# When queries are turned and multiplied by the tangent, in a linear-attention and Swish kernel: two steps moved, and five smaller pieces of work shared out anew

## The chip, the cores and the metric

The kernel runs on one core of one Trainium2 chip. The metric is device time in microseconds for one execution. Before the change the median of 5 runs is 277.74 us (277.08 to 279.45).

## What is computed

Attention without a softmax, then a feed-forward layer with a Swish whose slope is given per feature. Cut to what matters:

```python
# q, k, v: (8 batches, 8 heads, 576 positions, 64), w_in 512x2048, w_out 2048x512
theta = np.pi / 2.0 * pos / S                 # c = cos(theta), s = sin(theta)
phi = lambda x: np.concatenate([relu(x) * c, relu(x) * s], axis=-1)
q_p, k_p = phi(q), phi(k)
kv = np.einsum('bhsf,bhsd->bhfd', k_p, v);  z = np.sum(k_p, axis=2)
num = np.einsum('bhsf,bhfd->bhsd', q_p, kv)
den = np.einsum('bhsf,bhf->bhs', q_p, z)[..., None] + 1e-06
x = (num / den)                               # laid out as (4608 tokens, 512)
h = x @ w_in
g = h * (1.0 / (1.0 + np.exp(-beta * h)))
out = g @ w_out
```

The kernel takes the cosine out of num and den, so that a query needs only its ReLU and, for the second half of the features, its ReLU times the tangent.

## The kernel before, in words

The 4608 tokens are nine chunks c of 512; the attention works by batches b of 576 tokens. While chunk c goes through the feed-forward layer, the attention of batch b = c + 1 is finished, and its result becomes part of the input of the next chunk. The products with `w_in` and `w_out` are mostly done in the seven-product form for two by two blocks (`h_fast` at L459 and `o_fast` at L534), which needs sums of blocks beforehand: `g_sum` (L390, tiles S) over the activations, `wh_sums` (L439) over blocks of `w_in`, `x_sum` (L901) over blocks of the chunk's input.

Each engine runs its own queue in program order and waits on semaphores. No scheduler reorders anything: the order is that of the Python calls. In chunks 3 to 8 it is a list written out by hand, `ORDER` (L874) for chunks 3 to 6, read word by word by `chunk` (L930). Words that matter here:

- `c5X` is VectorE's copy of a partial product (L494); `kt` its copy of the key-value product into `kv` (L284); words with `a`, such as `a2Y` or `a3Y`, are VectorE's additions in PSUM (L496 to L498); `SaX`, `SbV` and the like are ScalarE's Swish activations of a pair of feature blocks (L413).
- `s01` to `s34` are VectorE's S sums (L399).
- `N0` is TensorE's numerators of batch b (L293), then `x0` to `x2` divide them (L304 to L315) and turn the result with a transposing DMA on SyncE's queue (L363).
- `q0` and `q1` are the ReLU of the queries of batch b + 2 into the one buffer `qb` (L194). `k`, `v` and `w` words are the ReLU of keys and the products of values by sine (ScalarE, L217) and cosine (VectorE, L219) for batch b + 1.
- `g0` and `g1` are GpSimd's two tangent products (L222, `q_tan`): the queries turned by DMA, `qts[b % 2]`, times the tangent.
- The queries of a batch are turned by one DMA of 18 blocks of 128x128, issued by SyncE (L252, `q_turn_dma`). It reads `qb` and writes `qts[b % 2]`.

GpSimd's queue also issues the stores of the output (L510, `store`), and SyncE's queue all loads (L79), the query turns and the turns of x.

Chunks 0 and 1 are a plain loop over 16 feature blocks (slots) with side work hung on slots (`early`, L736, and the loop at L809). Chunk 2 has its own order (`h_first`, L989, and the loop body from L1012), and ends with products named by `x[...]` and `y[...]`, where `y["a7"]` is VectorE's addition at L599 and `y["4"]` the last product, which goes on in the PSUM bank that `a7` reads.

The seven products of one pair in `o_fast` use three PSUM banks, and each is waited for by ScalarE's or VectorE's copy of what it left:

```python
"7": lambda: prod(b_ps, s_part(S3), T3, False, False, late(c)),
"4": lambda: prod(b_ps, g_part(1, 1), T4, False, True, late(c)),
"c1": lambda: nc.scalar.copy(p1, b_ps),
"a7": stored("2a7", lambda: nc.vector.tensor_tensor(o2[:, HM:DM], b_ps, p5, **add)),
```

Of the kernel before, what the change touches and what calls it, by code (L numbers as in the profile page):

```python
# [17 lines left out]
NQ = 9  # L18
# [4 lines left out]
def kernel(  # L23
# [14 lines left out]
    nc = tc.nc  # L38
# [154 lines left out]
        else:  # L193
            nc.vector.tensor_scalar(dst, src, scalar1=0.0, scalar2=None, op0=ALU.max)  # L194

    def q_relu(b, jp, eng="dve"):
        relu(qb[:, jp].rearrange("q n (j d) -> q j n d", j=2), raw_tile(b, "q")[:, 2 * jp : 2 * jp + 2], eng)

    def k_relu(b, j0=0, j1=4, eng="dve", n0=0, n1=NQ):
        relu(rk.rearrange("q n j d -> q j n d")[:, j0:j1, n0:n1], raw_tile(b, "k")[:, j0:j1, n0:n1], eng)  # L200
# [47 lines left out]
    def qs_of(b):  # L248
        return wx["q"] if b > 3 and b % 2 == 0 else qs_first

    def q_turn_dma(b):
        nc.sync.dma_start(out=qts[b % 2].rearrange("q s n c -> q (s n) c"),  # L252
                          in_=qb.rearrange("q s n c -> q (s n c)"), transpose=True)

    def q_tan(b, jp, behind=None):
        got = tan_mul(nc.gpsimd, qs_of(b)[:, jp], qts[b % 2][:, jp], 0, NQ)

        if behind is not None:
            tc.add_manual_dep(got.ins, behind.ins.name,
                              mybir.DependencyInfo(mybir.DependencyClass.Sync, mybir.DependencyReason.DATA),  # L260
                              reason="GpSimd behind the sums")

    def kv_out(jp, bank):
        return ps[:, bank : bank + 2, jp * 2 * E : (jp + 1) * 2 * E]
# [120 lines left out]
    def h_act(c, jt):  # L385
        if (c, jt // 4) not in gs:
            gs[c, jt // 4] = gt_pool.tile([P, 4, TCH], BF16, name="g_t", tag="g_t")
        nc.scalar.activation(gs[c, jt // 4][:, jt % 4], ps[:, h_bank(c, jt)], AF.Silu, scale=beta[:, jt : jt + 1])  # L388

    def g_sum(c, i0, i1, kind):  # L390

# [13 lines left out]

    def h_group(c, jt, cols=1):
        h_mm(c, jt, cols=cols)
        h_act(c, jt)

    def h_silu(c, jt, bank):  # L410
        if (c, jt // 4) not in gs:
            gs[c, jt // 4] = gt_pool.tile([P, 4, TCH], BF16, name="g_t", tag="g_t")
        nc.scalar.activation(gs[c, jt // 4][:, jt % 4], ps[:, bank], AF.Silu, scale=beta[:, jt : jt + 1])  # L413

    def h_plain(c, jt, bank, cols=1):
        xt = xt_tile(c)
# [276 lines left out]
    def rest():  # L693

        cast_halves(2)
        cast_halves(3)
        x_mul(x_rden(2, 0, 8, NQ, (0, 1)), 8, NQ)
        load_w("out", 0)
        load_w("out", 1)
        load_raw(1, "v")  # L700
        load_raw(1, "k")
        load_raw(1, "q")
        load_w("out", 2, 2)
        load_w("out", 3, 2)
        x_turn_dma(0, 8, 9)
        for j in range(8):
            cast_out(j)
        v_scale(1, 0)
        k_relu(1)
        q_relu(1, 0)  # L710
        q_relu(1, 1)


    def num_seven(jp, bank):
# [5 lines left out]
    def second():  # L720
# [14 lines left out]

    early = {  # L736
        4: lambda: (num_mm(0, 8, 0, 2, 0), num_mm(0, 8, 1, 2, 1), rest()),
        15: lambda: v_scale(1, 1, eng="act"),
        22: lambda: (kv_mm(1, 0, 6), kv_mm(1, 1, 6), kv_take((0, 1), 6, "act")),
        23: second,  # L740
        25: lambda: (num_seven(0, 4), x_mul(x_rden(4, 0, 0, 7, (0,)), 0, 7), cast_out(13)),
        26: lambda: (num_seven(1, 6), x_mul(x_rden(6, 0, 0, 7, (1,)), 0, 7)),
# [28 lines left out]
        if b + 1 < B:  # L771
            load_raw(b + 1, "k")

    def kv_all(b, bank=6):
        kv_mm(b, 0, bank)
        kv_mm(b, 1, bank)
        kv_take((0, 1), bank)

    def x_part(b, t, bank):
        x_div(t, bank)  # L780
# [30 lines left out]
    for slot in range(16):  # L811
        h_group(1, slot)
        if slot == 0:
            num_rest()
            att_q(2)
            v_half(2, 0)
        if 3 <= slot < NQ:
            v_half(2, 1, slot, slot + 1, "act")
        if slot == 4:
            k_all(2)  # L820
            v_half(2, 1, 0, 3)
        elif slot == 6:
            w_sums()
        elif slot == 11:
            kv_all(2)
            for jp in range(2):
                tan_mul(nc.vector, qs_of(2)[:, jp], qts[0][:, jp], 0, NQ)
    q_relu(3, 0, "act")
# [38 lines left out]
    def k_piece(b, j):  # L867
# [4 lines left out]
            load_raw(b + 1, "k")  # L872

    ORDER = (  # L874
# [6 lines left out]
    ORDER_LAST = (  # L881
# [42 lines left out]
    def chunk(c, b, x, y, parts):  # L924
        steady = {"X": (0, 2, 0, 1), "Y": (4, 3, 4, 5), "Z": (8, 0, 2, 1), "V": (12, 4, 3, 5)}
        end = {"X": (0, 6, 0, 1), "E": (2, 5, 3, 4), "Y": (4, 2, 0, 1), "F": (6, 7, 3, 4), "Z": (8, 6, 0, 1),
               "V": (12, 5, 3, 4)}
        pairs = {n: h_fast(c, at[0], at[1:]) for n, at in (steady if b < B else end).items()}

        def plain_bank(n):  # L930
            return (2 if n == 7 else 6 + n % 2) if b < B else (2, 7)[n % 2]

        plain = [2, 3, 6, 7, 10, 11, 14, 15]
        outs = {"x": x, "y": y}

        def q_next():
            if b + 3 < B:
                load_raw(b + 3, "q")

        def raw_next(name):  # L940
            if b + 2 < B:
                load_raw(b + 2, name)

        xs_all = {"x0", "x1", "x2"}
        take = prep(b, [
            ({"k0", "k1", "k2", "k3"} | xs_all, lambda: raw_next("k")),
            ({"q0", "q1"} | xs_all, q_next),
            ({f"{o}{n}" for o in "vw" for n in range(NQ)}, lambda: raw_next("v"))])
        last_sum = None
        for op in (ORDER if b < B else ORDER_END if c + 1 < NTC else ORDER_LAST).split():  # L950
            n = int(op[-1]) if op[-1].isdigit() else None
            if op == "K":
                kv_mm(b, 0, 4)
                kv_mm(b, 1, 4)
            elif op == "kt":
                kv_take((0, 1), 4)
            elif op[0] == "N":
                for t, bank in enumerate(parts):
                    num_all(b, t, bank)
            elif op[0] == "x":  # L960
                x_part(b, n, parts[n])
                take(op)
            elif op[0] in "kvwq":
                take(op)
            elif op[0] == "t":
                if c + 1 < NTC:
                    x_sum(c + 1, n)
            elif op[0] == "g":
                if b + 1 < B:
                    q_tan(b + 1, n, None if n else last_sum)  # L970
            elif op[0] == "p":
                h_plain(c, plain[n], plain_bank(n), 2 if n < SPLITS.get(c, (0, 0))[0] else 1)
            elif op[:2] == "sp":
                h_silu(c, plain[n], plain_bank(n))
            elif op[0] == "o" and n is not None:
                outs[op[1]][op[2]]()
            elif op[0] == "o":
                outs[op[2]]["a" + op[1]]()
            elif op[0] == "c" and op[2] in "xyo":
                outs["x" if op[2] == "o" else op[2]][op[:2]]()  # L980
            elif op[0] == "s":
                last_sum = g_sum(c, 2 * int(op[1]), 2 * int(op[1]) + 2, n)
            else:
                pair = op[0] if op[0] in pairs else op[-1]
                pairs[pair][op.replace(pair, "")]()
        if b + 2 < B:
            q_turn_dma(b + 2)

    def h_first(c):  # L989
        b = c + 1  # L990
        for slot in range(16):
            h_group(c, slot, 2 if slot < SPLITS.get(c, (0, 0))[0] else 1)
            if c == 2:
                if slot == 0:
                    k_all(b)
                    v_half(b, 1, 0, 4)
                if 1 <= slot < 6:
                    v_half(b, 1, slot + 3, slot + 4, "act")
                if slot == 3:
                    att_q(b + 1)  # L1000
                    wh_sums(4)
                if slot == 9:
                    wh_sums(8)
            if slot == (8 if c == 2 else 1):
                kv_all(b)
            if slot in (3, 7, 11):
                g_sums(c, slot // 2 - 1, slot // 2 + 1)
            elif slot in (13, 15):
                sums = g_sums(c, slot // 2, slot // 2 + 1)
        return sums  # L1010

    FAST = 3  # L1012
    for c in range(2, NTC):
# [4 lines left out]
        if c >= FAST:  # L1018
            chunk(c, b, x, y, parts)
            continue  # L1020
        sums = h_first(c)
        for t, bank in enumerate(parts):
            num_all(b, t, bank)
        q_tan(b + 1, 0, sums)
        q_tan(b + 1, 1)
        for i, n in enumerate("156273"):
            x[n]()
            if n in "156":
# [15 lines left out]
        y["c5"]()  # L1044
        if c == FAST - 1:
            x_sums(c + 1)
            wh_sums(12)
        v_half(b + 1, 1, 2, 3, "act")
        y["6"]()
        y["cu"]()  # L1050
# [5 lines left out]
        y["3"]()  # L1056
        y["a3"]()
        v_half(b + 1, 0, 7, 9)
        v_half(b + 1, 1, 3, 9, "act")
        y["4"]()  # L1060
        y["c4"]()
        q_turn_dma(b + 2)


# [28 lines left out]
```

## Time and profile before

| what | value |
|---|---|
| median of 5 runs | 277.74 us (277.08 to 279.45) |
| the profiled execution | 277.29 us, of which the span from first to last instruction is 275.5 us |
| TensorE busy | 268.2 us, 97% of the span |
| VectorE, ScalarE, GpSimd busy | 220.9, 184.6 and 67.8 us |
| granted TensorE clock, mean | 0.998 |
| DMA | 54.00 MB, 196 GB/s over the span |

The chunks begin on TensorE about at 19 us (chunk 0), 50 (1), 80 (2), 109 (3), 137 (4), 165 (5), 193 (6), 221 (7) and 246 (8).

How to read it: PE is TensorE's matmul and PEld its weight load, DVE is VectorE, ACT ScalarE, POOL GpSimd, SPq SyncE's queue. L399 is line 399 of the kernel before. In a timeline a row is a start, a duration, an engine, a line, an operation, the tile written and the tiles read, and a count when equal instructions follow each other; a bracket at its end tells how long the engine idled before it and what ended that. In a table of stretches each engine has its busy time and its number of instructions in that stretch.

### The profile page before, as it was taken

The numbers are of one execution on the slowest core, as the hardware profiler recorded it, in microseconds if no ns is written. First come the engines' busy times: TensorE is split into PE (matmuls) and PEld (weight loads), VectorE is DVE, ScalarE is ACT, GpSimd is POOL, SyncE is SP. The second block draws the span as 40 slices with busy tenths as digits, with TensorE's granted clock in tenths as the row PEclk, the third lists the DMA queues.
The fourth block names the chain that finished last, engine by engine and source line by source line (L and its number), as shares of the span: only waits on it lengthen the run. The fifth ranks groups of instructions, "written<-read, shape, count | busy, mean of one in ns | idle before, by whom it ended". The sixth has DMA issues, their size and how long they took to land.

```text
span 275.5 us, 9047 instructions
## 1 busy us (share of the span) xinstructions
PE 268.2 (97%) x3749; PEld 199.4 (72%) x3749; DVE 220.9 (80%) x578; ACT 184.6 (67%) x381; POOL 67.8 (25%) x87
## 2 busy tenths in 40 slices
PE   8899999999999999999999999999999999999993
PEld 8454455446875599869866998688668886888683
DVE  5989978599999898599959995899589589558851
ACT  5778757797248657796669756986694289429821
POOL 1444000600087083106420552044300140000000
PEclk9999999999999999999999999999999999999999
DMA  6999999999969999971899198915400740033005
GB/s 228 376 394 384 391 389 315 382 195 379 245 157 306 244 305 298 396 132 40 177 361 269 36 220 278 145 21 107 114 2 12 117 115 2 0 69 87 2 24 130
DMA packets 50745, 54.00 MB, mean 196 GB/s; under 512 B 31232, under 2 KB 31760, under 8 KB 50704
## 3 DMA queue, kind: packets, MB, share of 16 engines
q1 hardware_dynamic: 47744, 45.88, 59.4%
q0 software_dynamic: 2688, 7.34, 9.2%
q8 instruction: 29, 0.48, 0.7%
q10 hardware_dynamic: 272, 0.21, 0.3%
q14 instruction: 12, 0.10, 0.1%
HBM read 36.71 MB, written 9.44 MB: 167 GB/s over the span
## 4 chain that ended last, share of the span: by engine, by line
PE 86%; DMA 7%; DVE 2%; SPq 1%; ACT 1%; issue 1%; ACTq 0%; DVEq 0%
PE ps L547 31%; PE ps L468 16%; PE ps L380 14%; PE ps L422 13%; DMA raw_v<-in_v_dram 7%; PE ps L517 5%; PE ps L293 3%; PE ps L272 3%; SPq L79 1%; ACT vb L217 1%; DVE xs L315 1%; PE ps L234 0%; PE ps L352 0%; DVE win L115 0%; ACT o_sb L567 0%
## 5 line engine op out<-in xcount | busy, mean ns | idle before, releaser
L413 ACT ACTIVATE g_t<-ps,beta 128x512 bf16<-128x512 f32 x96 | 61.0, 698 | 3.0 <-DVE ps L498 2.8
L547 PEld LDWEIGHTS <-S 128*128 128x128 bf16 x589 | 51.3, 98 | 5.0
L510 POOL DMA_DIRECT2D out_dram<-o_sb x56 | 33.6, 605 | 66.4 <-ACT o_sb L523 24.7
L380 PE MATMUL ps<-xt,win 128*128 128x512 bf16 (+1 forms) x196 | 42.8, 375 | 0.1
L547 PEld LDWEIGHTS <-g_t 128*128 128x128 bf16 x440 | 38.2, 98 | 4.3 <-issue 0.3
L422 PE MATMUL ps<-xt,win 128*128 128x512 bf16 (+1 forms) x184 | 40.8, 351 | 0.0
L388 ACT ACTIVATE g_t<-ps,beta 128x512 bf16<-128x512 f32 x48 | 32.1, 689 | 8.0 <-PE ps L380 7.9
L380 PEld LDWEIGHTS <-win 128*128 128x128 bf16 x196 | 18.7, 98 | 21.2 <-issue 0.6
L547 PE MATMUL ps<-wout,g_t 128*128 128x256 bf16 (+1 forms) x284 | 31.7, 262 | 0.0
L547 PE MATMUL ps<-wout,S 128*128 128x256 bf16 (+1 forms) x305 | 31.5, 255 | 0.0
L547 PE MATMUL ps<-T,S 128*128 128x256 bf16 (+1 forms) x284 | 30.8, 262 | 0.0
L217 ACT ACTIVATE vb<-raw_v,sin 128x256 bf16<-128x256 f32 (+1 forms) x61 | 27.4, 501 | 1.1 <-DMA raw_v<-in_v_dram 1.0
L399 DVE TENSOR_TENSOR S<-g_t 128x512 bf16<-128x512 bf16 (+1 forms) x66 | 25.1, 409 | 3.6 <-ACT g_t L413 2.7
L222 POOL TENSOR_TENSOR qs<-qt,tanr 128x1152 bf16<-128x1152 bf16 x6 | 14.2, 2385 | 50.8 <-DVE den L304 29.7
L468 PEld LDWEIGHTS <-w_stage 128*128 128x128 bf16 x224 | 21.6, 98 | 6.8
L468 PE MATMUL ps<-w_stage 128*128 128x256 bf16 x168 | 26.2, 272 | 0.0
L422 PEld LDWEIGHTS <-win 128*128 128x128 bf16 x184 | 17.9, 98 | 10.2
L315 DVE TENSOR_TENSOR xs<-ps,rden 128x768 bf16<-128x768 f32 (+4 forms) x26 | 22.8, 884 | 0.8
L219 DVE TENSOR_SCALAR vb<-raw_v,cos 128x256 bf16<-128x256 f32 x63 | 20.5, 379 | 0.0
L468 PEld LDWEIGHTS <-win 128*128 128x128 bf16 x168 | 16.4, 98 | 4.8 <-issue 0.3
L468 PE MATMUL ps<-xt,win 128*128 128x256 bf16 x112 | 19.1, 273 | 0.0
L594 ACT COPY p<-ps 128x256 f32<-128x256 f32 x16 | 6.0, 372 | 16.9 <-PE ps L547 16.9
(105 smaller groups left out, 416.6 us busy)
## 6 DMA issues: line engine op xcount, KB each, us to landing
raw_v<-in_v_dram SPq DMA_DIRECT2D x7, 1152.0 KB, 10.1
raw_k<-in_k_dram SPq DMA_DIRECT2D x7, 1152.0 KB, 7.4
raw_q<-in_q_dram SPq DMA_DIRECT2D x7, 1152.0 KB, 8.0
out_dram<-o_sb POOLq DMA_DIRECT2D x56, 128.0 KB, 4.3
w_stage<-in_moe_w_in_dram SPq DMA_DIRECT2D x3, 1024.0 KB, 13.0
w_stage<-in_moe_w_out_dram SPq DMA_DIRECT2D x2, 1024.0 KB, 7.9
w_stage<-in_moe_w_out_dram SPq DMA_DIRECT2D x4, 512.0 KB, 12.0
out_dram<-o_sb SPq DMA_DIRECT2D x12, 128.0 KB, 2.4
```

Of the source, the lines that this page charges most:

```text
L217: nc.scalar.activation(o, a, AF.Copy, scale=t[:, n : n + 1])
L219: nc.vector.tensor_scalar(o, a, scalar1=t[:, n : n + 1], scalar2=None, op0=ALU.mult)
L222: return eng.tensor_tensor(dst.rearrange("q n (g p) -> q n g p", g=2), src.rearrange("q n (g p) -> q n g p", g=2), tanr[:, n0:n1].unsqueez ...
L315: nc.vector.tensor_tensor(o.rearrange("q j n s d -> q j (n s) d"), nv[:, :, a:z, :, 0:D].rearrange("q j n s d -> q j (n s) d"), rden[:, :, ...
L380: nc.tensor.matmul(ps[:, h_bank(c, jt), i * 64 : (i + w) * 64], lhsT=win[jt // 4][:, mi, (jt % 4) * P : (jt % 4 + 1) * P], rhs=xt[:, i : i ...
L388: nc.scalar.activation(gs[c, jt // 4][:, jt % 4], ps[:, h_bank(c, jt)], AF.Silu, scale=beta[:, jt : jt + 1])
L399: return nc.vector.tensor_tensor(o, l, r, op=op)
L413: nc.scalar.activation(gs[c, jt // 4][:, jt % 4], ps[:, bank], AF.Silu, scale=beta[:, jt : jt + 1])
L422: nc.tensor.matmul(ps[:, bank, o * 64 : z * 64], lhsT=win[jt // 4][:, mi, (jt % 4) * P : (jt % 4 + 1) * P], rhs=xt[:, o:z, jp, g * HP : (g ...
L468: nc.tensor.matmul(dst, lhsT=left[:, g], rhs=right[:, :, g * HP : (g + 1) * HP], start=start and g == 0, stop=stop and g == 1, skip_group_ ...
L510: (eng or own).dma_start(out=out_v[bb, n][:, m0:m1], in_=o_sb[hf * HP : (hf + 1) * HP, m0:m1])
L547: nc.tensor.matmul(dst[:, m : m + w], lhsT=left(i), rhs=right[:, i, m : m + w], start=start and i == 0, stop=stop and i == order[-1], skip ...
```

## The change

Two steps move in chunks 3 to 6. The turn of the next batch's queries (`q_turn_dma`) leaves the end of the chunk before and stands at `N0`, with an explicit wait for the last Swish activation issued before it (`SbV`); so the turn for batches 5, 6 and 7 is issued at the numerators of chunks 3, 4 and 5, where it was issued at the ends of chunks 2, 3 and 4. GpSimd's tangent products for batches 4 to 7 leave the place behind the S sums of the chunk before and stand at the beginning of their own chunk, with an explicit wait for VectorE's copy `c5X`.

Five smaller edits go with it. In chunk 0, half of the ReLU of batch 1's keys and four ninths of half of its queries go from VectorE to ScalarE, and one value product comes back to VectorE. In chunk 1, two of six value products with the sine go from ScalarE to VectorE and the other four are issued a slot earlier. In chunk 1 the key-value product stands at slot 10 where it stood at slot 11, and its copy goes from VectorE to ScalarE. In chunk 2 `wh_sums(12)`, four VectorE sums, moves from before `y["6"]` to behind the value products near the end. The functions `h_act`, `h_group` and `h_silu` return their instruction.

```diff
-    def q_relu(b, jp, eng="dve"):
-        relu(qb[:, jp].rearrange("q n (j d) -> q j n d", j=2), raw_tile(b, "q")[:, 2 * jp : 2 * jp + 2], eng)
+    def q_relu(b, jp, eng="dve", n0=0, n1=NQ):
+        relu(qb[:, jp, n0:n1].rearrange("q n (j d) -> q j n d", j=2),
+             raw_tile(b, "q")[:, 2 * jp : 2 * jp + 2, n0:n1], eng)
...
-    def q_turn_dma(b):
-        nc.sync.dma_start(out=qts[b % 2].rearrange("q s n c -> q (s n) c"),
-                          in_=qb.rearrange("q s n c -> q (s n c)"), transpose=True)
-
-    def q_tan(b, jp, behind=None):
-        got = tan_mul(nc.gpsimd, qs_of(b)[:, jp], qts[b % 2][:, jp], 0, NQ)
-
+    def after(got, behind, reason):
         if behind is not None:
             tc.add_manual_dep(got.ins, behind.ins.name,
                               mybir.DependencyInfo(mybir.DependencyClass.Sync, mybir.DependencyReason.DATA),
-                              reason="GpSimd behind the sums")
+                              reason=reason)
+
+    def q_turn_dma(b, behind=None):
+        got = nc.sync.dma_start(out=qts[b % 2].rearrange("q s n c -> q (s n) c"),
+                                in_=qb.rearrange("q s n c -> q (s n c)"), transpose=True)
+        after(got, behind, "turn behind the activations")
+
+    def q_tan(b, jp, behind=None):
+        got = tan_mul(nc.gpsimd, qs_of(b)[:, jp], qts[b % 2][:, jp], 0, NQ)
+        after(got, behind, "GpSimd behind a copy")
...
         v_scale(1, 0)
-        k_relu(1)
+        v_scale(1, 1, n0=8)
+        k_relu(1, 0, 2)
         q_relu(1, 0)
-        q_relu(1, 1)
+        q_relu(1, 1, n1=5)
...
-        15: lambda: v_scale(1, 1, eng="act"),
-        22: lambda: (kv_mm(1, 0, 6), kv_mm(1, 1, 6), kv_take((0, 1), 6, "act")),
+        15: lambda: (v_scale(1, 1, n1=8, eng="act"), k_relu(1, 2, 4, "act")),
+        22: lambda: (kv_mm(1, 0, 6), kv_mm(1, 1, 6), kv_take((0, 1), 6, "act"), q_relu(1, 1, "act", 5)),
...
-        if 3 <= slot < NQ:
-            v_half(2, 1, slot, slot + 1, "act")
+        if 2 <= slot < 6:
+            v_half(2, 1, slot + 3, slot + 4, "act")
         if slot == 4:
             k_all(2)
-            v_half(2, 1, 0, 3)
+            v_half(2, 1, 0, 5)
...
-        elif slot == 11:
-            kv_all(2)
+        elif slot == 10:
+            kv_all(2, eng="act")
...
-        "p0 Y1 X1 c1X p1 X5 c5X sp0 X6 X2 K c1Y X3 cuX kt Y6 X7 p2 a2X a3X Y5 sp1 a7X cuY c5Y Y7 Z1 SaX "
+        "p0 Y1 X1 c1X p1 X5 c5X g0 g1 sp0 X6 X2 K c1Y X3 cuX kt Y6 X7 p2 a2X a3X Y5 sp1 a7X cuY c5Y Y7 Z1 SaX "
         "X4 c1Z p3 Y3 Y2 SbX sp2 a7Y Z2 s01 Y4 Z5 sp3 Z6 s03 a3Y a2Z p4 SbY V1 a2Y c5Z cuZ Z7 s02 a7Z p5 "
         "SaY c1V V6 Z3 s11 sp4 s12 cuV a3Z V2 Z4 s14 sp5 V5 SbZ c5V V7 p6 a2V V3 SaZ a7V a3V s21 sp6 SaV "
-        "p7 s04 s13 V4 s22 SbV s23 sp7 s24 s31 s33 N0 k1 s32 ox1 c1o ox5 k3 c5o k2 ox6 s34 g0 g1 x0 k0 "
+        "p7 s04 s13 V4 s22 SbV s23 sp7 s24 s31 s33 N0 k1 s32 ox1 c1o ox5 k3 c5o k2 ox6 s34 x0 k0 "
         "ox3 oy1 cuo c1y x2 o3x ox2 ox7 v8 oy5 x1 c5y o2x oy6 w8 q0 q1 cuy v2 v6 oy3 o7x v3 w1 oy7 w4 w3 "
...
-        last_sum = None
+        first = last = None
...
             elif op[0] == "N":
+                if b + 1 < B:
+                    q_turn_dma(b + 1, last)
                 for t, bank in enumerate(parts):
                     num_all(b, t, bank)
...
             elif op[0] == "g":
-                if b + 1 < B:
-                    q_tan(b + 1, n, None if n else last_sum)
+                if b < B:
+                    q_tan(b, n, None if n else first)
...
-                pairs[pair][op.replace(pair, "")]()
-        if b + 2 < B:
-            q_turn_dma(b + 2)
+                got = pairs[pair][op.replace(pair, "")]()
+                if op == "c5X":
+                    first = got
+                if op[:2] in ("Sa", "Sb"):
+                    last = got
...
-        sums = h_first(c)
+        h_first(c)
         for t, bank in enumerate(parts):
             num_all(b, t, bank)
-        q_tan(b + 1, 0, sums)
-        q_tan(b + 1, 1)
...
             x_sums(c + 1)
-            wh_sums(12)
         v_half(b + 1, 1, 2, 3, "act")
...
         v_half(b + 1, 0, 7, 9)
+        wh_sums(12)
         v_half(b + 1, 1, 3, 9, "act")
         y["4"]()
         y["c4"]()
-        q_turn_dma(b + 2)
```

More of the change, by code (lines that the diff above doesn't have):

```diff
@@ L387, in h_act @@
             gs[c, jt // 4] = gt_pool.tile([P, 4, TCH], BF16, name="g_t", tag="g_t")
-        nc.scalar.activation(gs[c, jt // 4][:, jt % 4], ps[:, h_bank(c, jt)], AF.Silu, scale=beta[:, jt : jt + 1])
+        return nc.scalar.activation(
+            gs[c, jt // 4][:, jt % 4], ps[:, h_bank(c, jt)], AF.Silu, scale=beta[:, jt : jt + 1])
     def g_sum(c, i0, i1, kind):
@@ L407, in h_group @@
         h_mm(c, jt, cols=cols)
-        h_act(c, jt)
+        return h_act(c, jt)
     def h_silu(c, jt, bank):
@@ L412, in h_silu @@
             gs[c, jt // 4] = gt_pool.tile([P, 4, TCH], BF16, name="g_t", tag="g_t")
-        nc.scalar.activation(gs[c, jt // 4][:, jt % 4], ps[:, bank], AF.Silu, scale=beta[:, jt : jt + 1])
+        return nc.scalar.activation(gs[c, jt // 4][:, jt % 4], ps[:, bank], AF.Silu, scale=beta[:, jt : jt + 1])
     def h_plain(c, jt, bank, cols=1):
@@ L772, in k_all, with kv_all @@
             load_raw(b + 1, "k")
-    def kv_all(b, bank=6):
+    def kv_all(b, bank=6, eng="dve"):
         kv_mm(b, 0, bank)
         kv_mm(b, 1, bank)
-        kv_take((0, 1), bank)
+        kv_take((0, 1), bank, eng)
     def x_part(b, t, bank):
@@ L981, in chunk @@
             elif op[0] == "s":
-                last_sum = g_sum(c, 2 * int(op[1]), 2 * int(op[1]) + 2, n)
+                g_sum(c, 2 * int(op[1]), 2 * int(op[1]) + 2, n)
             else:
                 pair = op[0] if op[0] in pairs else op[-1]
-                pairs[pair][op.replace(pair, "")]()
-        if b + 2 < B:
-            q_turn_dma(b + 2)
+                got = pairs[pair][op.replace(pair, "")]()
[3 more added lines that the diff above has]
+                    last = got
     def h_first(c):
@@ L1008, in h_first @@
             elif slot in (13, 15):
-                sums = g_sums(c, slot // 2, slot // 2 + 1)
-        return sums
+                g_sums(c, slot // 2, slot // 2 + 1)
     FAST = 3
```

## The prediction, made before the changed kernel was run

> **What bounds the kernel now.** I read the table of stretches first, one row a chunk.
>
> ```profile
> 0.00:32.00 32.00, 29.04 (x409) 17.80 (x410) 26.93 (x67) 23.06 (x43) 10.69 (x21) 1.00 0.97 352
> ...
> 92.00:109.00 17.00, 16.86 (x348) 14.57 (x347) 15.54 (x48) 11.36 (x25) 7.06 (x6) 1.00 1.16 268
> 109.00:137.00 28.00, 28.00 (x434) 23.22 (x432) 22.62 (x62) 20.56 (x44) 9.31 (x10) 1.00 0.69 192
> 137.00:165.00 28.00, 28.00 (x473) 22.44 (x471) 23.24 (x64) 20.96 (x45) 9.39 (x11) 1.00 0.82 222
> 165.00:193.00 28.00, 28.00 (x430) 22.67 (x428) 23.62 (x70) 20.96 (x45) 8.90 (x11) 1.00 0.64 140
> 193.00:221.00 28.00, 28.00 (x419) 21.81 (x417) 20.52 (x56) 15.60 (x33) 4.19 (x9) 1.00 0.31 60
> ...
> 246.00:275.50 29.50, 25.26 (x214) 20.61 (x211) 16.99 (x46) 16.27 (x37) 0.00 (x0) 0.98 0.27 63
> ```
>
> The first busy time in a row is TensorE's: 28.00 of 28.00 us in chunks 3 to 6, where the two steps move. Its 7.3 us of idle time lie before 32 us (2.96) and in the tail (4.24), which no edit touches, and 0.14 before chunk 3. "Busy" can hide a stall, so I also took the distance from each matmul's start to the next against the usual one of its shape (109 ns for 256 columns): behind 20 us only one exceeds it by over 0.2 us, by 0.31, at 107.69. The kernel is bound by TensorE's own work, and the change takes no matmul away. The timeline there:
>
> ```profile
> 106.33 0.28 DVE L445 TENSOR_TENSOR w_stage<-win 128x256 bf16<-128x256 bf16 x1
> ...
> 107.05 0.29 DVE L448 TENSOR_TENSOR w_stage<-win,w_stage 128x256 bf16<-128x256 bf16 x1
> 107.26 0.41 DVE L597 TENSOR_TENSOR o_sb<-ps,p 128x256 f32<-128x256 f32 x1
> 107.59 0.41 DVE L599 TENSOR_TENSOR o_sb<-ps,p 128x256 f32<-128x256 f32 x1
> 107.70 0.10 PEld L547 LDWEIGHTS <-g_t 128*128 128x128 bf16 x1
> ...
> 108.06 1.05 PE L547 MATMUL ps<-T,g_t 128*128 128x256 bf16 x15
> ```
>
> The four sums of wh_sums(12) hold VectorE from 106.33 to 107.34; the addition L599 (`a7`) ends at 108.01, and product `4` starts 0.05 us later.
>
> **The parts.** *wh_sums(12) later:* L597's matmuls end at 106.13 and L599's at 107.02, so without the sums L599 runs at about 107.07 and ends at 107.49, before the weights are in at 107.80. TensorE gains the 0.31 us. The sums (0.93 us) go behind the last value product, about 109.0 to 110.0, into VectorE's 2.16 us of idle time before the copy at 111.55; their tile is needed only by the last pair's product, seven us on. Late next would be ScalarE's copies, at usual distances. Gain 0.2 to 0.31; I take 0.31.
>
> *Chunk 0:* half of the keys' ReLU on ScalarE starts when the keys land at 36.2 and takes about 1.2 us (four pieces of half its size took 2.40), so 37.4, before the product at 37.99. The split queries end at 40.35 on VectorE against 40.65, and on ScalarE (free at 40.23) at about 40.8, when the transposes, today 0.15 us late, need them. ScalarE is then some 0.25 us later; the tightest user has 0.24 us (a weight cast, used at 42.09). Between -0.15 and +0.15: taken as 0. *Chunk 1:* two more value products on VectorE (0.54 us) end at about 59.2; the product one slot earlier is at 60.4. ScalarE's copy falls between two activations, and its banks are released 1.3 to 3.2 us before use. 0.
>
> *Tangent products:* each chunk has two of 2.38 us, 4.73 together. They read and write nothing that TensorE needs before N0, 11 us later; GpSimd's stores in front of them are issued by 111.5, and no store follows before 130. They cost something only where they hold VectorE, and they do:
>
> ```profile
> 33.37 2.44 DVE L219 TENSOR_SCALAR vb<-raw_v,cos 128x256 bf16<-128x256 f32 x9
> ```
> ```profile
> 76.50 4.72 POOL L222 TENSOR_TENSOR qs<-qt,tanr 128x1152 bf16<-128x1152 bf16 x2 [21.04 <-PE ps L547]
> ```
> ```profile
> 79.36 4.11 DVE L219 TENSOR_SCALAR vb<-raw_v,cos 128x256 bf16<-128x256 f32 x9
> ```
>
> The same nine products take 2.44 us alone and 4.11 when GpSimd is at its products until 81.2. Additions from PSUM aren't slowed (0.41 us under it and without). The new place is from about 112.1 (c5X ends at 111.97; GpSimd started 0.1 to 0.25 us behind its releaser elsewhere) to 116.8 or 116.95. VectorE in that time:
>
> ```profile
> 111.55 0.42 DVE L494 COPY p<-ps 128x256 f32<-128x256 f32 x1 [2.16 <-PE ps L468]
> 113.14 0.70 DVE L284 CAST kv<-ps 128x520 bf16<-128x520 f32 x1 [1.17 <-PE ps L272]
> ...
> 116.46 0.76 DVE L399 TENSOR_TENSOR S<-g_t 128x512 bf16<-128x512 bf16 x2 [0.52 <-ACT g_t L413]
> 117.14 0.42 DVE L498 TENSOR_TENSOR ps<-ps,u 128x256 f32<-128x256 f32 x1
> ```
>
> All reads PSUM until the S sums at 116.46, which have both inputs in SBUF. By the rows alone, no sum ever ran under GpSimd, so nothing tells; free is possible. The Trainium skill ("SBUF — State Buffer", Who interferes with whom) speaks against the place: a VectorE instruction with two SBUF inputs contends with a GpSimd instruction that reads SBUF, and the later one waits in full. By that rule the sums wait 0.3 to 0.5 us in each of chunks 3 to 6 (4.49 us from c5X to the sums in chunks 3, 4 and 5). I follow the rule, as the tensor_scalar rows show such a lock. Behind the sums wait the additions L498 and L496; then the activation at 118.28 (0.05 us behind L496), then ScalarE's copy that ends at 119.33, for a matmul at 119.78. That is 0.45 us of room, and VectorE has 0.24 us idle at 119.12. So TensorE loses 0 to 0.1 us a chunk, taken as 0.025, 0.1 in four. If nothing hid it: 4 x 0.5 = 2.0. The place given up costs VectorE 0.2 us today (0.55 for 0.34 at 130.90), hidden.
>
> *The turn:* SbV runs at 123.48 to 124.16, so the turn is issued at 124.2. Its cost is bounded by its own rows:
>
> ```profile
> DMA to landing us min/median/max: 6.3/10.4/13.9
> ```
>
> 6.3 is the turn at 68.85, whose issue held SyncE 4.38 us; 12.2 to 13.9 are those at chunk starts, issued 0.5 us behind a load of 1.15 MB and beside stores. At 124.2 all loads have landed (the last at 119.56) and so have the stores (117.8); I take 6.4: landed at 130.6. Queued behind it on SyncE: x0's turn, at 127.69 today, goes at 128.6; the third turn, at 130.99, by 0.2 later; its user on VectorE at 134.94 has 0.8 us. The new wait: q0 overwrites qb, so VectorE holds at 131.37 until the turn has landed, 0.8 us to spare. At the chunk's start loads and stores lose a rival, which no engine waits for. 0.
>
> **Sum.** 277.29 - 0.31 + 0.10 = 277.08, for the profiled execution. Three of the five runs lie at 277.1 to 277.7, and the profile is of these; the median is 0.45 above it. I predict 277.1, 0.2% under the median; a measurement of this kernel can tell about 0.5% (1.4 us).
>
> **Rivals.** *The turn lands late* (the slower side). If it takes the median 10.4 us it lands at 134.6, VectorE holds q0 for 3.2 us, with the addition L599 of 132.71 behind it, whose matmul at 134.34 has 1.23 us. TensorE then stands 2.0 us in each of chunks 3, 4 and 5: 283.1. It decides from 8.4 us upward (131.37 + 1.23 - 124.2). For it: four of six turns took longer. Against: all of these ran beside loads. 12 in 100. *kt waits for GpSimd:* no CAST ran under a tangent product. If it did wait for the first one's end (114.45), VectorE would be 1.3 us late at 114.31, where the next matmul has 0.25: 1.05 us in four chunks, 281.3. Against: it advances 520 elements in 0.62 us, [...]like the additions that aren't slowed, and the skill ("VectorE: DVE Perf Modes", Mode 2×_2P) gives the two-port mode to SBUF operands alone, so by the rule 0. 6 in 100. *The sums' wait passes on in full:* 277.29 - 0.31 + 2.0 = 279.0. 5 in 100, half of it past the bound. *The upper two runs (279.2 and 279.5) come from turns beside loads:* in chunk 5 the turn landed at 180.50 and the products began at 182.69, 2.2 us of room; a later landing would push them over VectorE's value products. Then the median falls, but not below TensorE's sum: 276.8, and past 0.5% only if the profile misses some time. 12 in 100, 5 of these faster by over 0.5%. The forecast itself: 65 in 100.
>
> So faster 0.05, same 0.74, slower 0.21. The range: 276.4 to 279.6; above it lie most of the two slower rivals (17), below it 2.
>
> **What would show it.** Right: L599 ends near 107.5 and product `4` follows at the usual distance; chunks 3 to 6 keep 28.0 us of TensorE; the S sums begin near 116.8 counted alike; the three turns land 6 to 7 us after issue and q0 isn't held. Wrong: idle time of TensorE behind L599, L498 or kt in these chunks.

## The result, and the profile after

The changed kernel takes 277.79 us (median of 44 runs, 276.73 to 281.1). The kernel before, run beside it, takes 278.62 us (79 runs, 277.08 to 281.27; the five runs shown first had 277.74). The ratio is 0.9973, 95% interval 0.996 to 0.9986: 0.27% faster, about 0.75 us, and the interval leaves 1 outside. The forecast was a time that can't be told from before.

The two profiled executions do not show this gain: 277.33 us with a span of 275.6 after, 277.29 with 275.5 before. The execution profiled before was a good one, 1.3 us under the median of its kernel; that of after is 0.5 under its own. So the gain lies in what differs between executions, and that needed other runs to see. First, what the profile after tells. The table of stretches:

```profile
0.00:32.00 32.00, 29.52 (x411) 18.20 (x412) 27.02 (x68) 23.27 (x44) 10.72 (x21) 1.00 0.97 353
32.00:66.00 34.00, 33.73 (x449) 17.27 (x448) 27.09 (x56) 26.09 (x46) 4.74 (x8) 1.00 1.05 335
...
92.00:109.00 17.00, 16.82 (x348) 14.59 (x346) 14.88 (x44) 11.15 (x25) 2.22 (x4) 1.00 1.11 255
109.00:137.00 28.00, 28.00 (x433) 23.24 (x431) 23.29 (x65) 20.63 (x44) 9.05 (x10) 1.00 0.74 203
137.00:165.00 28.00, 28.00 (x472) 22.43 (x471) 23.27 (x64) 21.04 (x45) 9.18 (x11) 1.00 0.81 223
165.00:193.00 28.00, 28.00 (x430) 22.68 (x428) 23.73 (x70) 21.05 (x45) 8.89 (x11) 1.00 0.57 137
```

TensorE, the first busy time, is still at 28.00 of 28.00 where the two steps moved. Its 0.27 us of idle time between 32 and 66 us is a wait for the ReLU of batch 1's queries, which follows their landing and began at 39.27 (39.22 before): TensorE lost 0.48 us less ahead of 32 us and so came to the same load earlier. Between 92 and 109 its idle time is no smaller than before, although the stall behind `a7` is gone, as the timeline there shows (line numbers are now 4 or 5 higher, so `a7` is L604 and the product L552):

```profile
106.83 0.41 DVE L602 TENSOR_TENSOR o_sb<-ps,p 128x256 f32<-128x256 f32 x1
107.39 0.42 DVE L604 TENSOR_TENSOR o_sb<-ps,p 128x256 f32<-128x256 f32 x1
...
108.02 1.05 PE L552 MATMUL ps<-T,g_t 128*128 128x256 bf16 x15
...
109.16 0.28 DVE L450 TENSOR_TENSOR w_stage<-win 128x256 bf16<-128x256 bf16 x1
```

`a7` ends at 107.81, product `4` follows at the usual distance, and the sums of `wh_sums(12)` run from 109.16. The time saved there was lost 12 us earlier, in the numerators of batch 3, as TensorE's own timeline shows:

```profile
95.79 0.20 PE L297 MATMUL ps<-kv,qt 64*64 64x65 bf16 x2
96.17 0.22 PE L297 MATMUL ps<-kv,qt 64*64 64x65 bf16 x2 [0.18 <-issue]
...
96.48 1.05 PE L552 MATMUL ps<-wout,g_t 128*128 128x256 bf16 x8
```

Four equal matmuls fall apart into two and two with 0.37 us from the last start to the next, and the bracket names no engine and no transfer: "issue". Before, the same row was `95.95 0.23 ... x4`, unbroken. Such a stage takes 1.36 to 1.39 us undisturbed, from its first matmul to the first one behind it; here it took 1.73.

The sums S in chunk 3, and the turns in chunks 3 to 5 (rows of the tile `qt`, with the times from issue to landing):

```profile
116.42 0.94 DVE L404 TENSOR_TENSOR S<-g_t 128x512 bf16<-128x512 bf16 x2 [0.53 <-ACT g_t L418]
```
```profile
L259 SPq DMA_TRANSPOSE qt<-qb x3: 2697/3244/3313, 124.2 to 180.4; - x3
...
DMA to landing us min/median/max: 5.2/5.3/5.4
```

GpSimd's products run from 112.02 to 116.74. The two sums take 0.94 us where they took 0.76: the wait is 0.18 (0.22 to 0.25 in chunks 4 to 6). The turns, the first issued at 124.22, land 5.2 to 5.4 us after their issue, where the same three landed after 12.2, 12.9 and 13.9.

### The profile page after: what moved, and what is told of

Same layout as the page of the kernel before. It is cut to its first block, busy times and chain, and to the rows that moved or that the text cites. A ratio compares the mean times of both kernels' runs of the same rounds, so it can differ in the third digit from the quotient of the medians.

```text
span 275.6 us, 9048 instructions
## 1 busy us (share of the span) xinstructions
PE 268.4 (97%) x3749; PEld 199.8 (73%) x3749; DVE 220.7 (80%) x580; ACT 186.2 (68%) x381; POOL 67.4 (24%) x87
## 4 chain that ended last, share of the span: by engine, by line
PE 84%; DMA 10%; SPq 3%; DVE 2%; issue 0%; ACTq 0%; ACT 0%; DVEq 0%
PE ps L552 36%; PE ps L473 16%; PE ps L427 13%; PE ps L384 10%; DMA raw_q<-in_q_dram 6%; DMA w_stage<-in_moe_w_in_dram 4%; PE ps L297 4%; PE ps L522 3%; PE ps L276 2%; SPq L79 2%; DVE win L115 1%; SPq L103 0%; PE ps L235 0%; PE ps L356 0%; DVE qb L194 0%
## 5 line engine op out<-in xcount | busy, mean ns | idle before, releaser
L552 PEld LDWEIGHTS <-S 128*128 128x128 bf16 x589 | 51.4, 98 | 5.0
L552 PEld LDWEIGHTS <-g_t 128*128 128x128 bf16 x440 | 38.2, 98 | 4.1
L552 PE MATMUL ps<-wout,g_t 128*128 128x256 bf16 (+1 forms) x284 | 31.7, 262 | 0.0
L552 PE MATMUL ps<-wout,S 128*128 128x256 bf16 (+1 forms) x305 | 31.5, 255 | 0.0
L552 PE MATMUL ps<-T,S 128*128 128x256 bf16 (+1 forms) x284 | 30.8, 262 | 0.0
L404 DVE TENSOR_TENSOR S<-g_t 128x512 bf16<-128x512 bf16 (+1 forms) x66 | 26.1, 423 | 3.6 <-ACT g_t L418 2.7
L218 ACT ACTIVATE vb<-raw_v,sin 128x256 bf16<-128x256 f32 (+1 forms) x58 | 25.9, 502 | 1.7 <-DMA raw_v<-in_v_dram 1.7
```

The lines of the kernel that those rows point to most:

```text
L218: nc.scalar.activation(o, a, AF.Copy, scale=t[:, n : n + 1])
L404: return nc.vector.tensor_tensor(o, l, r, op=op)
L552: nc.tensor.matmul(dst[:, m : m + w], lhsT=left(i), rhs=right[:, i, m : m + w], start=start and i == 0, stop=stop and i == order[-1], skip ...
```

## The experiments

Three sets of four kernels, each set on one chip, beside the kernel before on that chip. Kernels of one set can be compared directly, those of different sets by their ratios to before. The expectations name theories by letters: most of the gain comes from the place of the sums (A), from the moved turn and tangent products (B), or from chunks 0 and 1 (C). Theory D came after the first set; theory E is that the executions differ for some other reason.

### First set: each part alone

`e1_sums_later` is the kernel before with nothing but

```diff
             x_sums(c + 1)
-            wh_sums(12)
...
         v_half(b + 1, 0, 7, 9)
+        wh_sums(12)
```

> The kernel before with one part of the change: wh_sums(12) behind the value products. Theory A (the load of batch 4's values lands late in many executions, and the four sums of 0.93 us stood between that landing and the addition that TensorE waits for, so the part is worth 0.3 us in a good execution and up to 0.9 in a late one): 0.4 to 0.75 us faster, product 4 of chunk 2 not waiting for L599. Theory B (the moved turn and tangent products gain, by freeing the chunk starts): 0.3 us faster, as in the profile, and no more. Theory C (the pieces shared out anew in chunks 0 and 1): 0.3 us faster and no more.

Measured: 278.87 us (12 runs), ratio 1.0009 (0.9983 to 1.0036). `a7`'s stall is gone here too, and yet the profiled execution took 279.36 us. TensorE around 96 us:

```profile
96.17 0.20 PE L293 MATMUL ps<-kv,qt 64*64 64x65 bf16 x2
97.91 0.22 PE L293 MATMUL ps<-kv,qt 64*64 64x65 bf16 x2 [1.55 <-issue]
97.92 0.24 PE L293 MATMUL ps<-kv,qs 64*64 64x65 bf16 x4
```

This is the same stop as in the changed kernel, 22 matmuls before the end of the numerators, and now 1.74 us long. The inputs of the matmul that is held are tiles that the matmuls ahead of it had read already. So one edit of 0.31 us is drowned by a stop that comes and goes, and theory A, which asked for 0.4 to 0.75 us faster, falls. The stops account for the length of this execution: it is 2.07 us longer than the one profiled before; its numerators took 2.59 longer in all (table below) and the stall of 0.31 is gone, which makes 2.28.

`e2_turn_tan_only` has the two moves and not the five smaller edits.

```diff
+                if b + 1 < B:
+                    q_turn_dma(b + 1, last)
...
-                    q_tan(b + 1, n, None if n else last_sum)
+                    q_tan(b, n, None if n else first)
...
-            q_turn_dma(b + 2)
```

> The kernel before with the turn at the numerators and the tangent products at the beginning of their own chunk, all else as before. Theory A: within 0.2 us of the kernel before, since TensorE waits for neither. Theory B: 0.4 to 0.7 us faster. Theory C: within 0.2 us. All: the product behind L599 in chunk 2 still waits; the first S sums of chunks 3 to 6 take 0.15 to 0.25 us longer.

Measured: 277.75 us (12 runs), ratio 0.9983 (0.9959 to 1.0007). The stall behind `a7` is there and took 0.58 us. The median is 0.56 us under that of before, as theory B has it, but the interval includes 1.

`e3_early_edits_only` has the edits in chunks 0 and 1 alone.

```diff
-        k_relu(1)
+        v_scale(1, 1, n0=8)
+        k_relu(1, 0, 2)
         q_relu(1, 0)
-        q_relu(1, 1)
+        q_relu(1, 1, n1=5)
...
-        elif slot == 11:
-            kv_all(2)
+        elif slot == 10:
+            kv_all(2, eng="act")
```

> The kernel before with the edits of chunks 0 and 1 alone. Theory A: 0 to 0.15 us faster (the transposes of batch 1's queries wait 0.15 us less behind the load). Theory B: the same. Theory C: 0.4 us faster or more.

Measured: 278.17 us (12 runs), ratio 0.9991 (0.9967 to 1.0015); the 0.4 us or more of theory C are not seen.

`e4_after_sums_back` is the changed kernel with the sums in their old place.

```diff
             x_sums(c + 1)
+            wh_sums(12)
...
-        wh_sums(12)
```

> The changed kernel with wh_sums(12) put back before y 6. Theory A: within 0.25 us of the kernel before, so 0.4 to 0.75 of the gain is gone. Theory B or C: still 0.4 us faster than before.

Measured: 277.69 us (12 runs), ratio 0.9973 (0.9949 to 0.9997): the changed kernel's own, so the sums are hardly what makes the difference. Its profile has 0.61 us of standstill in chunk 2's numerators and 0.25 behind `a7`.

### Theory D: TensorE's instructions arrive late

In the changed kernel, `e1` and `e4` the stop falls on the same matmul, with no data to wait for. The profile lists two DMA queues of the kind "instruction", which the kernel doesn't issue. This is the larger one in the changed kernel (packets, MB, share):

```profile
q8 instruction: 29, 0.48, 0.8%
```

In the trace these are blocks of 16384 bytes, 3.5 to 17 us apart from chunk 0 on, and one comes just ahead of chunk 2's numerators. Its start against the moment at which TensorE goes on, with the longest time from one matmul's start to the next:

| kernel | block starts | TensorE goes on | later by | longest gap |
|---|---|---|---|---|
| before | 92.34 | not held | | none |
| after | 93.49 | 96.17 | 2.68 | 0.37 |
| e4 | 93.90 | 96.49 | 2.59 | 0.61 |
| e1 | 95.24 | 97.91 | 2.67 | 1.74 |

The later the block, the longer the gap, and the distance stays. In the other ten profiles kept from these runs and in that of before, TensorE came to this matmul 2.7 to 4.3 us after the block's start and wasn't held. Theory D: TensorE reaches the end of the instructions it holds and waits for this block, which waits in the DMA rings behind other transfers, a query turn above all. This is the turn of batch 4 on SyncE's queue in chunk 2, in the kernel before and in the changed one:

```profile
87.20 5.33 SPq L252 DMA_TRANSPOSE qt<-qb  x1
```
```profile
87.12 6.07 SPq L259 DMA_TRANSPOSE qt<-qb  x1
```

Its issue ends at 92.53 and 93.19; the block starts at 92.34 and 93.49. In `e4` and `e1` it starts 0.9 and 1.2 us behind the end of that issue, with two loads issued in between.

The numerators fit this: they take 288 instructions (144 weight loads, 144 matmuls) in 1.38 us, and a block of 16 KiB holds 256 by the Trainium skill ("Runtime: NRT & Kernel Launch", Instruction fetch mechanics), so a stage uses up more than one. The trace agrees when TensorE's instructions are counted: between the first block and the last of the kernel before there are 254 to a block on average (7123 in 28), and the stops seen in chunks 1, 2, 3 and 5 of all these kernels stand 767, 1025 and 1792 instructions apart, within one of 3, 4 and 7 times 256.

By this theory the moved turns matter in the same way: at the chunks' beginnings they ran beside loads for 12 to 14 us, over the block that chunk 3's numerators need (121.75 us in before).

### Second set: where a turn may stand

`f1_chunk2_turn_later` moves the one turn of chunks 2 to 5 that still runs beside loads ahead of numerators, that of batch 4 in chunk 2, to the numerators. The ReLU of batch 5's queries, which overwrites the buffer that the turn reads, goes behind five value products.

```diff
-                    att_q(b + 1)
+                    att_q(b + 1, False)
...
-        h_first(c)
+        q_turn_dma(b + 1, h_first(c))
         for t, bank in enumerate(parts):
...
-        att_q(b + 2, False)
         y["1"]()
         v_half(b + 1, 0, 0, 5)
+        att_q(b + 2, False)
```

> The changed kernel with the same step taken in chunk 2: the turn of batch 4 issued at that chunk's numerators, behind its last activation, and the ReLU of batch 5's queries behind five value products. Theory D (executions differ because TensorE stands still in the numerators of chunk 2 until its next block of instructions has come, 16 KB on queue 8, and that block comes late when the turn and a load are in the rings ahead of it; seen at 95.8 as 0 to 1.7 us): no such stall in the profile, the block starts before 92.5, the slowest executions disappear, and the median is 0.3 to 0.8 us under the changed kernel's 277.8 (so 0.996 to 0.993 of the kernel before). Theory E (the executions differ for another reason, say the first 20 us or the load of batch 4's values): within 0.2 us of the changed kernel. If the ReLU waits for the turn, a stall near 104 to 106 instead.

Measured: 277.33 us (12 runs, 276.62 to 277.9), ratio 0.9945 (0.9923 to 0.9966), the fastest of the kernels so far; its interval just touches the changed kernel's. The block starts at 92.37; the turn is issued at 95.78 and has landed 5.7 us later. TensorE in the stretch that held the stop:

```profile
92.00:109.00 17.00, 17.00 (x350) 14.65 (x348) 15.12 (x46) 11.65 (x26) 3.63 (x5) 1.00 0.99 229
```

17.00 of 17.00, where the changed kernel has 16.82. The edit does one thing more: with the turn out of the way, SyncE issues the next load of queries at 87.28 and not at 93.27. No run tells what that is worth alone.

`f2_turn_six_earlier` issues the turns of chunks 3 to 5 six microseconds before the numerators, all loads having landed.

```diff
-                if op[:2] in ("Sa", "Sb"):
+                if op == "SbY":
                     last = got
```

> The changed kernel with the three turns issued about 6 us earlier, behind SbY instead of SbV (about 118.2, 146.3 and 174.3), so that they are in the rings when the instructions of the numerators are fetched (121.6, 147.3 and 177.8). Theory D: a stall of 0.3 to 2 us in the numerators of at least one of chunks 3 to 5 and a median 0.3 to 2 us above the changed kernel. Theory E: the same as the changed kernel, since no engine waits for a turn that lands earlier.

Measured: 279.12 us (12 runs), ratio 1.0025 (0.9999 to 1.0051), 0.5% above the changed kernel's. The turns are as fast as in the changed kernel (5.0 to 6.2 us to landing), so what they cost is their place. TensorE in chunk 5:

```profile
180.88 0.22 PE L297 MATMUL ps<-kv,qt 64*64 64x65 bf16 x4
182.27 0.23 PE L297 MATMUL ps<-kv,w_stage 64*64 64x65 bf16 x4 [1.17 <-issue]
```

The turn ran from 174.71 to 180.4. The block that started at 177.76 in the changed kernel starts at 179.83, 1.8 us late when the 0.3 us are taken off that TensorE was behind by then, and TensorE goes on 2.44 us after its start. A turn holds blocks back even without a load beside it; "all loads have landed" isn't what makes the new place good, "behind the block" is.

`f3_turn_back` is the changed kernel with the three turns at the chunks' ends again; the products stay.

```diff
-                if b + 1 < B:
-                    q_turn_dma(b + 1, last)
...
+        if b + 2 < B:
+            q_turn_dma(b + 2)
...
         y["c4"]()
+        q_turn_dma(b + 2)
```

> The changed kernel with the three turns back at the ends of chunks 2, 3 and 4; the tangent products stay at the beginning of their own chunk. Theory D, if what the moved turn gains is a free ring for instructions: 0.3 to 0.5 us slower than the changed kernel (0.998 to 0.9995 of the kernel before), with late blocks or a stall in the numerators of chunks 3 to 5. If the tangent products' place gains instead: the same as the changed kernel.

Measured: 278.19 us (12 runs), ratio 0.9983 (0.9957 to 1.0009); the numerators of chunks 3 and 5 take 1.61 and 1.49 us in its profile. It is 0.4 us above the changed kernel (0.1% by the ratios), which the intervals don't separate.

`f4_three_products` puts the lock's price to the test: the second tangent product is done twice, with the same result, in chunks 3 to 6.

```diff
                     q_tan(b, n, None if n else first)
+                    if n:
+                        q_tan(b, n)
```

> The changed kernel with the second tangent product of each of chunks 3 to 6 done twice (the same values to the same place), so that GpSimd is at it until about 119.1. It measures the lock alone. If the rule on two SBUF inputs holds: the first S sum, due at 116.42, ends 0.2 to 0.3 us behind GpSimd, at 119.3; TensorE, which had 0.45 us of room, stands 1.5 to 2.5 us in each of four chunks: 284 to 288. If the sums are only slowed: 278.

Measured: 284.65 us (4 runs), ratio 1.0201 (1.0153 to 1.0249). Its timeline in chunk 3:

```profile
116.04 3.12 DVE L404 TENSOR_TENSOR S<-g_t 128x512 bf16<-128x512 bf16 x2 [0.52 <-ACT g_t L418]
...
119.08 0.42 DVE L503 TENSOR_TENSOR ps<-ps,u 128x256 f32<-128x256 f32 x1
...
119.56 0.38 PE L473 MATMUL ps<-xt,win 128*128 128x256 bf16 x2 [1.33 <-DVE ps L503]
```

The sums now wait 2.36 us, until GpSimd is done at 118.88, and TensorE waits for the addition behind them in each of four chunks. So the sums are held to the end of GpSimd's product: 2.4 us more of GpSimd's work cost about 6.9 us in four chunks (284.65 less 277.79), 1.7 in each. With two products the same wait is 0.2 us and stays inside the room that the prediction counted.

### Third set: each part taken back from the best version

`g0_f1_again` repeats `f1_chunk2_turn_later`, beside the other three.

> f1 once more, as the base of the three beside it: it differs little from one execution to the next, so parts of the change can be told in it. All theories: 277.1 to 277.6, and no execution above 278.5.

Measured: 276.95 us (12 runs), ratio 0.9954 (0.9928 to 0.998).

`g1_f1_turns_back` has the three turns at the chunks' ends.

```diff
-                if b + 1 < B:
-                    q_turn_dma(b + 1, last)
...
+        if b + 2 < B:
+            q_turn_dma(b + 2)
...
+        q_turn_dma(b + 2)
```

> f1 with the turns of batches 5 to 7 back at the ends of chunks 2 to 4. Theory D: 0.1 to 0.4 us above g0, with the numerators of chunks 3 to 5 longer than 1.38 us in some chunk. If the moved turn is worth nothing once chunk 2 is free: equal to g0 within 0.1.

Measured: 277.69 us (12 runs), ratio 0.9991 (0.9963 to 1.002); 0.74 us above `g0_f1_again` (95%, by resampling the runs: 0.28 to 1.63), more than the 0.1 to 0.4 expected. Its profile has what the one profile of before did not catch, in chunk 3's numerators:

```profile
124.19 0.22 PE L297 MATMUL ps<-kv,w_stage 64*64 64x65 bf16 x2
125.78 0.22 PE L297 MATMUL ps<-kv,w_stage 64*64 64x65 bf16 x2 [1.38 <-issue]
```

The turn was issued at 109.59, its issue took 12.34 us and it landed at 125.40; the block started at 123.31 (121.38 in `g0_f1_again`) and TensorE went on 2.47 us later.

`g2_f1_sums_back` has the sums in their old place.

```diff
             x_sums(c + 1)
+            wh_sums(12)
...
-        wh_sums(12)
```

> f1 with wh_sums(12) back before y 6. If what the four sums cost is the 0.25 to 0.58 us seen behind the addition at the end of chunk 2: 0.2 to 0.6 us above g0 with that stall in the profile. If the earlier loads of f1 have given VectorE time there: equal to g0, and no stall.

Measured: 277.35 us (12 runs), ratio 0.9963 (0.9938 to 0.9988); 0.40 above `g0_f1_again` (-0.1 to 1.07), with a stall of 0.22 us behind `a7`.

`g3_f1_early_undone` has chunks 0 and 1 as before the change.

```diff
-        v_scale(1, 1, n0=8)
-        k_relu(1, 0, 2)
+        k_relu(1)
...
-        elif slot == 10:
-            kv_all(2, eng="act")
+        elif slot == 11:
+            kv_all(2)
```

> f1 with the edits of chunks 0 and 1 undone. As in e3: 0.1 to 0.2 us above g0, at the transposes of batch 1's queries. If they are worth nothing: equal within 0.1.

Measured: 277.11 us (12 runs), ratio 0.996 (0.9932 to 0.9987); 0.16 above `g0_f1_again` (-0.31 to 0.39). Its profiled execution was one of the two long ones (278.68), and only part of that is a stop in the numerators, of 0.66 us in chunk 1. It also stood 0.91 us behind `a7`, although the sums were out of the way:

```profile
107.10 0.43 DVE L459 TENSOR_TENSOR w_stage<-xt 128x512 bf16<-128x512 bf16 x1 [1.53 <-DMA xt<-xs]
...
108.91 0.41 DVE L604 TENSOR_TENSOR o_sb<-ps,p 128x256 f32<-128x256 f32 x1
...
109.38 1.05 PE L552 MATMUL ps<-T,g_t 128*128 128x256 bf16 x15 [0.75 <-DVE o_sb L604]
```

VectorE had waited 1.53 us for a turn of x. So a late transfer can reach TensorE by another way than its instructions.

How long the numerators took in the profile of each kernel (us from their first matmul's start to the start of the next product; 1.36 to 1.39 is undisturbed, in chunk 1 1.47, where the product behind them comes 0.1 later):

| kernel | chunk 1 | 2 | 3 | 4 | 5 |
|---|---|---|---|---|---|
| before | 1.53 | 1.36 | 1.38 | 1.38 | 1.38 |
| after | 1.47 | 1.73 | 1.48 | 1.38 | 1.39 |
| e1, sums moved | 2.02 | 3.10 | 1.74 | 1.38 | 1.38 |
| e2, turn and products | 1.61 | 1.36 | 1.38 | 1.38 | 1.39 |
| e3, early edits | 1.47 | 1.36 | 1.38 | 1.38 | 1.54 |
| e4, after, sums back | 1.47 | 1.97 | 1.38 | 1.38 | 1.38 |
| f1, best | 1.47 | 1.36 | 1.39 | 1.38 | 1.38 |
| f2, turns earlier | 1.47 | 1.36 | 1.67 | 1.38 | 2.74 |
| f3, turns back | 1.47 | 1.36 | 1.61 | 1.38 | 1.49 |
| f4, three products | 1.47 | 1.36 | 1.38 | 1.38 | 1.39 |
| g0, best again | 1.85 | 1.36 | 1.38 | 1.38 | 1.39 |
| g1, best, turns back | 1.47 | 1.36 | 2.97 | 1.38 | 1.39 |
| g2, best, sums back | 1.47 | 1.36 | 1.38 | 1.38 | 1.39 |
| g3, best, early undone | 2.00 | 1.36 | 1.39 | 1.39 | 1.45 |

Stops beyond 0.2 us in chunks 2 to 5 appear only where a turn runs ahead of the numerators, over the time at which their block is due; before's profile has such turns and happens to be without a stop in these chunks.

## Why the prediction was wrong

**The step that failed** is the last of *the turn*: "At the chunk's start loads and stores lose a rival, which no engine waits for. 0." TensorE itself waits for one of the transfers that stood there with the turn: not a load or a store, but the next block of its own program. With the turns at the chunks' beginnings this costs 0.4 to 0.75 us in the median: 0.74 in `g1_f1_turns_back` against `g0_f1_again`, the one pair whose interval keeps clear of zero; 0.17% or 0.5 in before against `e2_turn_tan_only`; 0.1% to 0.4 us in `f3_turn_back` against the changed kernel. It costs nothing in a good execution. That the executions of before that weren't profiled stop in the same way is inferred from these. The profile read for the prediction was a good one, so "behind 20 us only one exceeds it by over 0.2 us" was true of it and not of the kernel. A first sign lay just under that limit: in chunk 1's numerators of that profile two matmuls start 0.19 us apart, where 0.04 is the most in an undisturbed stage. The rule of the Trainium skill that bears on this ("Runtime: NRT & Kernel Launch", Instruction fetch mechanics) says that fetching is hidden, as instructions are dispatched slower than blocks arrive. By it the cost would be 0; the rows above show stops of 0.37 to 1.74 us, and the measurement decides. The prediction also took 0.5% as the least that a measurement of this kernel can tell; with 44 and 79 runs the interval is 0.26% wide, so a change of 0.27% is seen.

**The anchor** failed with it: "Three of the five runs lie at 277.1 to 277.7, and the profile is of these". With 79 runs the median is 278.62, so the profile was 1.3 us under it and not 0.45. The sum, 277.1, was of an execution almost without stops; the median after, 277.79, still contains some (chunk 2's numerators, 0.37 in its profile).

**The rival that came nearest** is *the upper two runs come from turns beside loads*. Turns beside loads are the cause, but the victim it named, late tangent products on VectorE, isn't: the stops are in TensorE's own queue. It was given 12 in 100.

**wh_sums(12)**: right. 0.31 was foretold, the stall was gone in the profile after, and with the sums in their old place the profiles show 0.22 to 0.58. In the median it can't be separated from nothing by these runs (0.40, -0.1 to 1.07). Nor does it guard that place against a late turn of x, as `g3_f1_early_undone` shows.

**Chunks 0 and 1**: taken as 0; measured 0.16 (-0.31 to 0.39) and, alone, ratio 0.9991. Right within what can be told.

**Tangent products**: right in kind and too large in size. The sums wait 0.18 to 0.25 us a chunk and not 0.3 to 0.5: the products ended at 116.74, somewhat earlier than reckoned, and the sums began at 116.42, as early as before. TensorE's loss, taken as 0.1 in all, is not to be seen. `f4_three_products` shows the wait that the rule foretold, with 2.36 us. The rival *kt waits for GpSimd* is refuted: the copy into `kv` ran in 0.70 us from 113.10, in the middle of a product.

**The turn's own time**: 6.4 us was taken, 5.3 measured, and `q0` wasn't held. *The turn lands late* is refuted. *The sums' wait passes on in full* is refuted too.

**The forecast** of 65 in 100 for "no visible change" rested on a sum without any term for what differs from run to run. The term that was missing is 0.4 to 0.75 us, up to 0.27% of the kernel. The range, 276.4 to 279.6, held the time, but it was wide enough to do so whatever the cause.

## What to carry to other kernels

Before you put a transfer's new place down at nothing, ask which instruction block TensorE needs next: a stage of many tiny matmuls uses up a block in little over a microsecond, and a large transposing DMA issued some microseconds ahead of it makes the block late. Put such a transfer behind the block that the stage needs, say beside the stage itself, as `f1_chunk2_turn_later` does: ratios of 0.9945 and, repeated, 0.9954 to before, where the changed kernel has 0.9973. And where one profile sits well below the median of the runs, look for gaps that end with "issue" in several profiles before you take its idle time for the kernel's.

## What the runs showed of the hardware

- A gap on TensorE that ends with "issue" can be a wait for instructions: it ended 2.4 to 2.7 us after the start of a 16 KB block on queue q8 in five profiled executions, whatever the gap's length (0.37 to 1.74 us). The block's own transfer took 1.0 to 1.2 us of that; the rest is not explained. That the block belongs to TensorE is inferred from this timing and from the count of instructions between stops; the trace doesn't name its engine.
- Blocks are late behind data. A query turn with no load beside it put one off by about 1.8 us (`f2_turn_six_earlier`, 177.76 to 179.83, less 0.3 by which TensorE itself was late); one with loads by 1.9 (`g1_f1_turns_back`, 121.38 to 123.31).
- The same turn of 18 blocks of 128x128 lands 4.9 to 6.2 us after issue when it is issued at the numerators of chunks 3 to 5 or six microseconds ahead of them, and after 10.5 to 15.8 at the chunks' beginnings, beside loads; SyncE is held 2.7 to 3.9 us by the one and 8.3 to 12.3 by the other.
- Chunk 1's numerators, at 68 us, stop for 0.2 to 0.7 us in five of the fourteen profiles (before, `e1`, `e2`, `g0`, `g3`). What holds their block wasn't tried and stays open.
- Open, too, is the exact split of the 0.75 us, which the intervals leave wide. The first 67 us also differ from one profile to the next (chunk 1's numerators begin at 67.40 to 68.11 us), and no run sets that apart. The granted clock is not the cause: it is 0.996 to 1.0 in nearly all runs, long and short ones alike.
